# State-space scan and gated FFN on one core: reordered start of chunk 0

## The chip, the cores and the metric

The kernel runs on one core of a Trainium2 chip. The metric is the device time of one execution in microseconds (us). TensorE (PE), VectorE (DVE), ScalarE (ACT), GpSimd (POOL) and SyncE (SP) each run their own queue in program order and wait for one another by semaphores.

## The reference

```python
# x: 4 batches, 8 heads, 768 tokens, head size 32; B, C: state size 16; a: decay per token
for c in range(nc):                      # chunks of 32 tokens
    cum = cumsum(log(clip(a)))           # within the chunk
    M = einsum('bhin,bhjn->bhij', C, B) * exp(cum_i - cum_j) * causal
    y = M @ x + (C @ state) * exp(cum_i)
    state = exp(sum(la)) * state + sum_j B_j x_j exp(cum_end - cum_j)
h = y_as_tokens_by_256 @ w_in            # 3072 x 256 by 256 x 2048
out = (h * cos(h)) @ w_out               # 3072 x 2048 by 2048 x 256
```

The result of the scan, 3072 tokens by 256, is the input of a feed-forward block with 2048 hidden columns. All is float32. The chunk of 32 in the reference is only a way to compute the recurrence; the kernel may cut the sequence otherwise.

## The kernel before

**Tiling.** The sequence of 768 tokens is cut into NC = 6 chunks of P = 128. In each chunk, the scan of all four batches gives yT, the transposed y, and the feed-forward block of that chunk runs in NF = 16 steps. While a chunk's steps run, the scan of the next chunk is interleaved with them. Chunk 0 has nothing to be interleaved with, so its scan is cut into two units, k = 0 and 1, of W = 64 tokens, and the feed-forward steps of chunk 0 take turns: the even steps work on unit 0, the odd ones on unit 1 (`turn_of`). Steps 2j and 2j + 1 use the same hidden columns.

**One step n of the feed-forward block.** `first(n)` multiplies yT by four 128x128 blocks of w_in into hp (a PSUM bank, tag "h", two of them; hp n can only start when the bank of n - 2 has been read for the last time). `wind(n)` computes k, the number of turns as an integer, on ScalarE (L670), and w, the rest of a turn, on VectorE (L672). `gate(n)` takes the sine on ScalarE (L677, called cos in the text since it is shifted by a quarter turn), `gated(n)` multiplies by hp into gT on VectorE (L682). `second(n)` adds gT times w_out into o (L726 in chunk 0); it is called two steps later.

**The weights.** They arrive as 64-bit words in pieces, eight of w_in ("in", i) and eight of w_out ("out", i), and must be turned into float32. `grade(which, i)` is the first half: ScalarE takes |x| of the high words (L231) and a scaled copy of the low words (L229, tile last), and GpSimd clips |x| (L232). With `later=True` it returns the L229 part as `rest`, so that it can be put elsewhere in ScalarE's queue. `join(which, i)` is the second half: two VectorE instructions (L244, L246) and an add on GpSimd into w_in or w_out (L254). Piece i of either matrix holds the 256 hidden columns from 256i on. In chunk 0 these belong to the steps 2i and 2i + 1.

**The scan of chunk 0.** For unit k and batch half p, `spread_a` copies the decays over partitions by a small product on TensorE (L346, tile a_ps), and `decays0` runs the decay scan on VectorE (L356, tile lam). `turn_c` and `turn_b` transpose C and B on TensorE (L376, L390; tile tp), and ScalarE copies the results out (L380, L391). `reach0` is one product and one scan for the decay from the unit's start (L396, L398). `inner` forms C times B (L415, tile g), `weights` multiplies by lam (L424, tile m), `weigh0` and `weigh_c` scale B and C on GpSimd (L363, L406). `finish0` forms y: the part from the old state in unit 1 (L440), the part within the unit (L448), and then the sums of the new state (L458); ScalarE copies y into yT (L468, L466), and later `take` copies the state out (L476).

**What sets the order.** The program runs under a manual schedule: each engine gets its instructions in the order in which the Python code calls them. The order of the start is written out by hand below the helpers (L818 to L850) and in `first_steps` (L917), which covers steps 0 to 3. From step 4 on, a loop calls `first`, `wind`, `grade`, `gate`, `join` and `gated` of each step, with the piece given by `piece` (L869), and the scan's work of later chunks by the table `plan`. The loads are issued from SyncE's queue in the order of the code; only the loads of C of chunk 0 go from ScalarE's. The clipped decays are written to DRAM by `clips` (L860) and read back spread over partitions (arow), and the loads of later chunks are queued behind this.

Of the kernel before, what the change touches and what calls it, by code (L numbers as in the profile page):

```python
# [25 lines left out]
def kernel(  # L26
# [12 lines left out]
    nc = tc.nc  # L39
# [4 lines left out]
    P = 128  # L44
# [9 lines left out]
    W = P // 2  # L54
# [67 lines left out]
    def load_b(k, s, eng=nc.sync):  # L122

        eng.dma_start(out=bs[s * W:(s + 1) * W, k].rearrange("p q (h n) -> p (q h) n", h=H),
                      in_=B[2 * s:2 * s + 2, :, k * W:(k + 1) * W, :]
                      .rearrange("b h i n -> i (b h) n"))
# [133 lines left out]
    fetch("in", 0)  # L260
    for s in range(2):
        load_x(0, s)
    for s in range(2):
        load_b(1, s)
    fetch("in", 1)
    for s in range(2):
        load_x(1, s)
# [9 lines left out]
    quarter = const.tile([P, 1], FP32, name="quarter")  # L277
    V.memset(quarter, HALF_PI)
    ACT.activation(const.tile([P, 1], FP32, name="sine"), quarter, AF.Sin)
    V.memset(a0z[:, :, 0:1], 0.0)  # L280
    for r in (slice(NB * H, W), slice(W, P)):
        V.memset(a0z[r, :, 1:], 0.0)
# [67 lines left out]
    def decays0(k, p, i=0, n=1):  # L350

        if p == i == 0:
            lams[k] = scan.tile([P, 2, H, W], FP32, tag="lam", bufs=4, name="lam")
        flat = "p h i -> p (h i)"
        hs = slice(i * H // n, (i + 1) * H // n)
        V.tensor_tensor_scan(out=lams[k][:, p, hs].rearrange(flat),  # L356
                             data0=spread.pop((k, p, i)).rearrange(flat),
                             data1=unit0[:, hs].rearrange(flat), initial=0.0,
                             op0=ALU.mult, op1=ALU.add)
# [12 lines left out]
    def turn_c():  # L372

        tp = bank([P, 4, P], "tp", "o")
        for r in range(4):
            PE.transpose(tp[:, r], c0[:, r].rearrange("p h n -> p (h n)"), ident)  # L376
        tp = tp.rearrange("p r (b k g) -> p k b g r", b=NB, k=2)

        def of(k, dst, **v):
            ACT.activation(dst.rearrange("p b (g r) -> p b g r", r=4), tp[:, k], AF.Copy, **v)  # L380

        def take(k):
            for t in range(2):
                of(k, cuts[k][:, t].rearrange("p q (s i) -> p (q s) i", s=2), scale=slot[:, t:t + 1])
        return take, of
# [16 lines left out]
    def weigh_c(k, of):  # L402
        c = scan.tile([P, NB, W], FP32, tag="rT", name="c1")
        of(k, c)
        rTs[k] = t = scan.tile([P, NB, W], FP32, tag="rT", name="rT")
        G.tensor_tensor(out=t, in0=c, in1=reach1[:, :, 1:], op=ALU.mult)  # L406
# [17 lines left out]
        V.tensor_tensor(out=m, in0=gs[k, q][:, :, 0:2 * P].rearrange("p k (s i) -> p k s i", s=2),  # L424
                        in1=l, op=ALU.mult)

    def finish0(k):

        m, xk = units[k], xrs[k]
        y = [pair("y") for _ in range(2)] if k else [pair("y")]  # L430
        at_ = [[(y[t][:, s, p * W:(p + 1) * W] if k else
                 y[0][:, s, t * P + p * W:t * P + (p + 1) * W]) for p in range(2)]
               for t in range(2) for s in range(2)]
        if k:
            old = states0.pop(k)
            for p in range(2):
                for s in range(2):
                    for q in range(4):
                        r, c0 = slice(32 * q, 32 * q + 32), W * (q % 2)
                        PE.matmul(at_[2 * (q // 2) + s][p][c0:c0 + W], lhsT=old[r, s, p],  # L440
                                  rhs=rTs[k][r, 2 * p + s], start=(p == 0), stop=False,
                                  tile_position=(32 * q, c0), skip_group_check=True)
        for p in range(2):
            for t in range(2):
                for s in range(2):
                    ss = slice(s * W, (s + 1) * W)
                    for q in range(4):
                        PE.matmul(at_[2 * t + s][p][32 * q:32 * q + 32],  # L448
                                  lhsT=xk[ss, p, 4 * t + q], rhs=m[ss, p, 4 * t + q],
                                  start=(k == p == t == 0), stop=True,  # L450
                                  tile_position=(s * W, 32 * q), skip_group_check=True)
        sc = scs.pop(k).rearrange("p (q k h) n -> p q k (h n)", q=2, h=2)
        x2 = xk.rearrange("p q (k h) d -> p q k (h d)", h=2)
        for p in range(2):
            for s in range(2):
                ss = slice(s * W, (s + 1) * W)
                for q in range(4):
                    PE.matmul(y[0][32 * q:32 * q + 32, s, 3 * P + p * W:3 * P + (p + 1) * W],  # L458
                              lhsT=sc[ss, p, q], rhs=x2[ss, p, q], start=False, stop=True,
                              tile_position=(s * W, 32 * q), skip_group_check=True)  # L460
        if k == 0:
            yT[0] = two.tile([P, 2, 2, 2 * P], FP32, tag="yT", name="yT")
        t_ = yT[0][:, k]
        if k:
            for t in range(2):
                ACT.copy(out=t_[:, t].rearrange("p (s i) -> p s i", s=2), in_=y[t][:, :, 0:P])  # L466
        else:
            ACT.copy(out=t_.rearrange("p t (s i) -> p s t i", s=2),  # L468
                     in_=y[0][:, :, 0:2 * P].rearrange("p s (t i) -> p s t i", t=2))
        states0[k + 1] = new = states.tile([P, 2, 2, 2 * D], FP32, tag="state0", bufs=2,  # L470
                                           name="state0")

        def take():
            for t in range(2):
                ts = slice(t * D, (t + 1) * D)
                ACT.activation(new[:, :, :, ts], y[0][:, :, 3 * P:].rearrange(  # L476
                    "p s (q d) -> p s q d", q=2)[:, :, :, ts], AF.Copy, scale=slot[:, t:t + 1])

        def add():
            dec = scan.tile([P, 2, 2, 2 * D], FP32, tag="whole", bufs=1, name="whole")  # L480
            r4 = reach1.rearrange("p (q s) i -> p s q i", s=2)
            for s in range(2):
                G.tensor_tensor(out=dec[:, s], in0=old[:, s],
                                in1=r4[:, s, :, W:].to_broadcast([P, 2, 2 * D]), op=ALU.mult)
            G.tensor_tensor(out=new, in0=new, in1=dec, op=ALU.add)
            for u in range(2):
                state[0, u] = new[:, u].rearrange("p s (t d) -> p s t d", t=2)
        return take, add
# [176 lines left out]
            if between and e == 0:  # L665
                between()

    def wind(n):
        k = ffn.tile([P, TB], I32, tag="k", name="k")
        ACT.activation(k, hp[n], AF.Copy, bias=0.25, scale=INV_2PI)  # L670
        turns[n] = w = ffn.tile([P, TB], FP32, tag="w", name="w")
        V.scalar_tensor_tensor(out=w, in0=hp[n], scalar=INV_2PI, in1=k,  # L672
                               op0=ALU.mult, op1=ALU.subtract)

    def gate(n):
        cos = turns[n]
        ACT.activation(cos, cos, AF.Sin, bias=quarter, scale=TWO_PI)  # L677
# [144 lines left out]
    spread_a(0, 1, 0, 2, "h")  # L822
    for p, i in ((0, 0), (0, 1), (1, 0)):
        decays0(0, p, i, 2)
    take_c, of_c = turn_c()
    tp_b = bank([P, 4, P], "tp", "o")
    take_b = turn_b(0, tp_b)
    spread_a(0, 1, 1, 2, "h")
    decays0(0, 1, 1, 2)
    take_c(0)  # L830
    take_b()
    scan_reach = reach0(1)
# [6 lines left out]
    for q in range(2):  # L839
        weights(0, q)  # L840
    take_c(1)
    weigh_c(1, of_c)
    join("in", 0)
    take_s0, _ = finish0(0)
    take_b = turn_b(1, tp_b)
    take_b()
    spread_a(1, 1, tag="o")
    inner(1, 0)
    for p in range(2):
        decays0(1, p)  # L850
# [66 lines left out]
    def first_steps():  # L917

        take_s0()
        first(0, lambda: inner(1, 1))  # L920
        weigh0(1)
        rest = grade("in", 1, later=True)
        rest()
        units_of_decay()
        for q in range(2):
            weights(1, q)
        wind(0)
        rest = grade("out", 0, later=True)
        take_s1, add_s1 = finish0(1)
        join("in", 1)  # L930
        first(1)
        gate(0)
        rest()
        clips()
        gated(0)
        wind(1)
        join("out", 0)
        first(2)
        rest = grade("in", 2, later=True)
        gate(1)  # L940
        take_s1()
        rest()
        gated(1)
        second(0)
        wind(2)
        join("in", 2)
        first(3)
        rest = grade("out", 1, later=True)
        gate(2)
        rest()  # L950
        gated(2)
        second(1)
        wind(3)
        join("out", 1)
        rest = grade("in", 3, later=True)
        gate(3)
        rest()
        gated(3)
        rest = grade("out", 2, later=True)
        join("in", 3)  # L960
        rest()
        return add_s1

    add_s1 = first_steps()
# [86 lines left out]
```

## Time and profile before

| | |
|---|---|
| time, median of 3 runs | 379.91 us (379.07 to 380.12) |
| span of the profiled execution | 376.4 us |
| PE busy | 366.0 us, 97% |
| PE weight loads busy | 325.2 us, 86% |
| DVE busy | 281.6 us, 75% |
| POOL busy | 215.6 us, 57% |
| ACT busy | 172.6 us, 46% |
| hp (L663), 768 records | 184.2 us |
| o in chunks 1 to 5 (L764), largest of its groups | 65.8 us |

The busy shares are means over the whole span. The page also gives the chain of work that ended last: 76% of the span on TensorE, 11% on SyncE's queue, 6% on VectorE. A line of the timeline gives start, length, engine, line, operation, output and inputs, the number of merged instructions and, in brackets, how long the engine stood idle before it and what released it.

### The profile page before, as it was taken

What the parts mean: (1) busy time and instruction counts of PE and PEld (TensorE: products, weight loads), DVE (VectorE), ACT (ScalarE), POOL (GpSimd) and SP (SyncE); (2) the same over time, 40 slices, a digit from 0 to 9 for tenths busy, and PEclk for the clock granted to TensorE, in tenths of its full rate; (3) what the DMA queues carried; (4) which work ended last, traced back from release to release, by engine and by line L of the source; (5) the groups of instructions that cost most, each with busy time, mean ns of one, the idle gap of its engine ahead of it and who ended that gap; (6) DMA issues with size and microseconds to landing.
All of it is one profiled execution on the core that took longest, in us unless ns stands there. A gap on an engine that the chain in (4) does not pass through costs nothing.

```text
span 376.4 us, 8678 instructions
## 1 busy us (share of the span) xinstructions
PE 366.0 (97%) x3272; PEld 325.2 (86%) x3272; DVE 281.6 (75%) x470; ACT 172.6 (46%) x293; POOL 215.6 (57%) x334
## 2 busy tenths in 40 slices
PE   8989999999999999999999999999999999999995
PEld 4567877888899899999899999999999989999995
DVE  6867999889889957987767987776887872554543
ACT  3677566535344334344433445433444443444442
POOL 5555775489947545684454694363775344554451
PEclk9999999999999999999999999999999999999999
DMA  7988988314536641845213653211020000010011
GB/s 130 259 245 234 254 209 161 84 14 120 138 82 85 123 109 16 127 111 136 39 31 35 122 151 84 46 19 17 2 39 9 10 21 2 2 29 2 2 28 28
DMA packets 121353, 31.54 MB, mean 84 GB/s; under 512 B 90496, under 2 KB 117216, under 8 KB 121312
## 3 DMA queue, kind: packets, MB, share of 16 engines
q1 hardware_dynamic: 120064, 30.60, 37.9%
q8 instruction: 26, 0.43, 0.5%
q10 hardware_dynamic: 1248, 0.39, 0.4%
q14 instruction: 15, 0.12, 0.1%
HBM read 27.64 MB, written 3.34 MB: 82 GB/s over the span
## 4 chain that ended last, share of the span: by engine, by line
PE 76%; SPq 11%; DVE 6%; DMA 3%; issue 2%; POOL 1%; ACT 1%; DVEq 0%; ACTq 0%
PE hp L663 36%; PE o L764 29%; SPq L110 6%; SPq L155 3%; PE o L726 3%; PE y L602 2%; PE g L560 2%; PE y L595 1%; DMA arow<-a_cut 1%; PE a_ps L346 1%; DVE lam L510 1%; DVE mag L246 1%; DVE gT L682 1%; DVE w L672 1%; PE warm L84 1%
## 5 line engine op out<-in xcount | busy, mean ns | idle before, releaser
L663 PE MATMUL hp<-yT,w_in 128*128 128x256 f32 x768 | 184.2, 382 | 3.9 <-DVE gT L682 1.9
L663 PEld LDWEIGHTS hp<-yT,w_in 128*128 128x128 f32 x768 | 139.0, 190 | 24.9 <-issue 6.8
L707 POOL TENSOR_TENSOR gd<-gT 128x256 f32<-128x256 f32 x79 | 59.2, 749 | 98.9 <-DVE gT L682 97.1
L677 ACT ACTIVATE w<-w,quarter 128x512 f32<-128x512 f32 x96 | 69.2, 721 | 80.8 <-DVE w L672 80.8
L672 DVE SCALAR_TENSOR_TENSOR w<-hp,k 128x512 f32<-128x512 f32 x96 | 65.4, 682 | 42.3 <-ACT k L670 42.1
L670 ACT ACTIVATE k<-hp 128x512 int32<-128x512 f32 x96 | 57.2, 595 | 83.8 <-PE hp L663 83.6
L682 DVE TENSOR_TENSOR gT<-hp,w 128x512 f32<-128x512 f32 x96 | 65.2, 679 | 33.2 <-ACT w L677 24.3
L764 PE MATMUL o<-words,gd 128*128 128x128 f32 x474 | 65.8, 275 | 0.0
L764 PEld LDWEIGHTS o<-words,gd 128*128 128x128 f32 x474 | 59.2, 192 | 0.0
L510 DVE TENSOR_TENSOR_SCAN lam<-arow,unit 128x512 f32<-128x512 f32 x40 | 56.6, 1414 | 0.0
L764 PEld LDWEIGHTS o<-w_out,gT 128*128 128x128 f32 x316 | 47.5, 191 | 4.0
L710 POOL TENSOR_TENSOR gd<-gT,gd 128x128 f32<-128x128 f32 x79 | 44.6, 565 | 6.2
L764 PE MATMUL o<-w_out,gT 128*128 128x128 f32 x316 | 48.0, 274 | 0.0
L709 POOL TENSOR_TENSOR gd<-gT,gd 128x128 f32<-128x128 f32 x79 | 44.2, 559 | 6.2
L726 PE MATMUL o<-w_out,gT 128*128 128x256 f32 x128 | 30.4, 381 | 1.0 <-POOL w_out L254 1.0
L581 DVE TENSOR_TENSOR m<-g,lam 128x256 f32<-128x256 f32 x80 | 30.9, 415 | 0.5
L764 PE MATMUL o<-w_out,gd 128*128 128x128 f32 x158 | 30.6, 275 | 0.0
L764 PE MATMUL o<-words,gT 128*128 128x128 f32 x158 | 30.5, 275 | 0.0
L726 PEld LDWEIGHTS o<-w_out,gT 128*128 128x128 f32 x128 | 24.1, 190 | 4.9 <-POOL w_out L254 1.8
L764 PEld LDWEIGHTS o<-w_out,gd 128*128 128x128 f32 x158 | 24.0, 192 | 0.0
L764 PEld LDWEIGHTS o<-words,gT 128*128 128x128 f32 x158 | 24.0, 192 | 0.0
L781 DVE TENSOR_TENSOR sum<-ps,sum 128x256 f32<-128x256 f32 (+1 forms) x27 | 16.7, 644 | 0.6
(108 smaller groups left out, 267.2 us busy)
## 6 DMA issues: line engine op xcount, KB each, us to landing
arow<-a_cut SPq DMA_DIRECT2D x20, 512.0 KB
words<-in_moe_w_in_dram SPq DMA_DIRECT2D x8, 512.0 KB
words<-in_moe_w_out_dram SPq DMA_DIRECT2D x8, 512.0 KB
out_dram<-sum SPq DMA_DIRECT2D x18, 128.0 KB
blocks<-in_B_dram SPq DMA_DIRECT2D x128, 8.0 KB
blocks<-in_C_dram SPq DMA_DIRECT2D x128, 8.0 KB
xr<-in_x_dram SPq DMA_DIRECT2D x14, 128.0 KB
along<-a_all SPq DMA_DIRECT2D x20, 64.0 KB
```

Source lines behind the costliest of these rows:

```text
L510: V.tensor_tensor_scan(out=lam[c, b][:, hs].rearrange("p h i -> p (h i)"), data0=rows_.rearrange("p h i -> p (h i)"), data1=unit[:, b % 2 ...
L581: V.tensor_tensor(out=m_[js, :, :, is_], in0=g_[js, :, :, is_], in1=l_[js, :, :, is_], op=ALU.mult)
L663: PE.matmul(to_[:, e], lhsT=w_in[:, k, fs], rhs=y[:, k], start=(k == 0), stop=(k == KT - 1), skip_group_check=True)
L670: ACT.activation(k, hp[n], AF.Copy, bias=0.25, scale=INV_2PI)
L672: V.scalar_tensor_tensor(out=w, in0=hp[n], scalar=INV_2PI, in1=k, op0=ALU.mult, op1=ALU.subtract)
L677: ACT.activation(cos, cos, AF.Sin, bias=quarter, scale=TWO_PI)
L682: V.tensor_tensor(out=gT[n], in0=hp.pop(n), in1=cos, op=ALU.mult)
L707: G.tensor_tensor(out=d[:, 0:2], in0=g[:, 1:2].to_broadcast([P, 2, P]), in1=g[:, 3::-3], op=ALU.subtract)
L709: G.tensor_tensor(out=d[:, 2], in0=g[:, 0], in1=d[:, 0], op=ALU.subtract)
L710: G.tensor_tensor(out=d[:, 3], in0=g[:, 2], in1=d[:, 2], op=ALU.subtract)
L726: PE.matmul(o[c, u][:, t], lhsT=g[:, 2 * e + t], rhs=w_out[:, 2 * j + e], start=(j == e == t == 0), stop=(j == NJ - 1 and e == 1), skip_gr ...
L764: PE.matmul(at[q], lhsT=a_[q], rhs=w[q], start=(j == 0 and q in starts), stop=(j == NJ - 1), skip_group_check=True)
```

## The change

It changes only the start: the scan of chunk 0 and the steps 0 to 3.

- In `finish0`, the sums of the new state come ahead of the part of y within the unit, which has to wait for m. A hook `between` lets the caller put work between these products and the copies into yT.
- In the order of the start, the last product `spread_a(0, 1, 1, ...)` and its scan come ahead of the transposes of C and B; `join("in", 0)` ahead of `weigh_c`; `spread_a(1, 1)` ahead of `turn_b(1)`.
- One of the four loads of B moves from SyncE's queue to ScalarE's.
- `wind` is split in its ScalarE and its VectorE half. In `first_steps`, the pieces are graded and joined earlier: out-1 is graded ahead of wind 2 instead of behind it, in-3 is graded in step 2 instead of step 3, and joined in step 3 ahead of the last part of out-2 instead of at the step's end.

```diff
-    for s in range(2):
-        load_b(1, s)
+    load_b(1, 0)
...
+    load_b(1, 1, nc.scalar)
...
-    def finish0(k):
+    def finish0(k, between=None):
...
+        sc = scs.pop(k).rearrange("p (q k h) n -> p q k (h n)", q=2, h=2)
+        x2 = xk.rearrange("p q (k h) d -> p q k (h d)", h=2)
+        for p in range(2):
+            for s in range(2):
+                ss = slice(s * W, (s + 1) * W)
+                for q in range(4):
+                    PE.matmul(y[0][32 * q:32 * q + 32, s, 3 * P + p * W:3 * P + (p + 1) * W],
+                              lhsT=sc[ss, p, q], rhs=x2[ss, p, q], start=(k == p == 0), stop=True,
+                              tile_position=(s * W, 32 * q), skip_group_check=True)
...
-                                  start=(k == p == t == 0), stop=True,
+                                  start=False, stop=True,
...
-        sc = scs.pop(k).rearrange("p (q k h) n -> p q k (h n)", q=2, h=2)
...
+        if between:
+            between()
...
+    spread_a(0, 1, 1, 2, "h")
+    decays0(0, 1, 1, 2)
     take_c, of_c = turn_c()
     tp_b = bank([P, 4, P], "tp", "o")
     take_b = turn_b(0, tp_b)
-    spread_a(0, 1, 1, 2, "h")
-    decays0(0, 1, 1, 2)
...
+    join("in", 0)
     weigh_c(1, of_c)
-    join("in", 0)
     take_s0, _ = finish0(0)
+    spread_a(1, 1, tag="o")
     take_b = turn_b(1, tp_b)
     take_b()
-    spread_a(1, 1, tag="o")
...
-        rest = grade("in", 1, later=True)
-        rest()
+        grade("in", 1)
         units_of_decay()
         for q in range(2):
             weights(1, q)
-        wind(0)
+        take_s1, add_s1 = finish0(1, lambda: wind_k(0))
+        join("in", 1)
+        wind_w(0)
+        first(1)
         rest = grade("out", 0, later=True)
-        take_s1, add_s1 = finish0(1)
-        join("in", 1)
-        first(1)
         gate(0)
         rest()
         clips()
         gated(0)
+        join("out", 0)
         wind(1)
-        join("out", 0)
         first(2)
         rest = grade("in", 2, later=True)
         gate(1)
...
         gated(1)
         second(0)
+        grade("out", 1)
+        join("in", 2)
         wind(2)
-        join("in", 2)
         first(3)
-        rest = grade("out", 1, later=True)
+        rest = grade("in", 3, later=True)
         gate(2)
+        join("out", 1)
         rest()
         gated(2)
         second(1)
         wind(3)
-        join("out", 1)
-        rest = grade("in", 3, later=True)
+        rest = grade("out", 2, later=True)
         gate(3)
+        join("in", 3)
         rest()
         gated(3)
-        rest = grade("out", 2, later=True)
-        join("in", 3)
-        rest()
```

More of the change, by code (lines that the diff above doesn't have):

```diff
@@ L449, in finish0 @@
                                   lhsT=xk[ss, p, 4 * t + q], rhs=m[ss, p, 4 * t + q],
-                                  start=(k == p == t == 0), stop=True,
+                                  start=False, stop=True,
                                   tile_position=(s * W, 32 * q), skip_group_check=True)
-        sc = scs.pop(k).rearrange("p (q k h) n -> p q k (h n)", q=2, h=2)
[L453 to L460, printed above, removed]
         if k == 0:
@@ L666, in first, with wind_k, wind_w @@
                 between()
-    def wind(n):
+    def wind_k(n):
         k = ffn.tile([P, TB], I32, tag="k", name="k")
         ACT.activation(k, hp[n], AF.Copy, bias=0.25, scale=INV_2PI)
+        turns[n] = k
+    def wind_w(n):
+        k = turns[n]
         turns[n] = w = ffn.tile([P, TB], FP32, tag="w", name="w")
@@ L673, in wind @@
                                op0=ALU.mult, op1=ALU.subtract)
+    def wind(n):
+        wind_k(n)
+        wind_w(n)
     def gate(n):
```

## The prediction

> **What bounds the kernel now.** I read the table of stretches first, because the page's averages mix a short start with a long steady part.
>
> ```profile
> core 0: us, PE busy (x) PEld busy (x) DVE busy (x) ACT busy (x) POOL busy (x), PEclk, DMA share, GB/s
> ...
> 10.00:20.00 10.00, 9.43 (x278) 6.39 (x277) 8.04 (x12) 6.74 (x16) 5.69 (x9) 1.00 1.00 281
> 20.00:30.00 10.00, 8.27 (x37) 6.50 (x36) 5.87 (x11) 6.95 (x14) 5.40 (x8) 1.00 0.87 229
> 30.00:40.00 10.00, 9.43 (x43) 7.70 (x42) 8.45 (x11) 5.64 (x10) 7.22 (x7) 1.00 0.81 216
> 40.00:50.00 10.00, 9.44 (x44) 7.71 (x43) 9.70 (x15) 7.43 (x13) 8.01 (x9) 1.00 0.93 249
> 50.00:60.00 10.00, 9.67 (x47) 8.23 (x46) 9.90 (x12) 5.51 (x10) 6.36 (x7) 1.00 0.84 208
> ```
>
> From 140 us on PE is full (59.94 of 60 us, then 99.95 of 100): nothing the diff edits lies there. Before that PE has holes: 0.57 us in 10-20, 1.73 in 20-30, 0.57, 0.56 and 0.33 in the next three. In 20-30 VectorE (DVE) is idle 4 us; from about 33 to 65 it is never free. So I read the start as three regimes: waits in a chain up to 33 us, VectorE from 33 to 65, TensorE after that. A microsecond won by 33 us comes out at the end only if both later regimes move up with it.
>
> Second view: the timeline, for which wait ends last at 25 to 37 us.
>
> ```profile
> 30.99 1.28 POOL L254 TENSOR_TENSOR w_out<-mag,last 128x512 uint32<-128x512 uint32 x1 [2.38 <-DVE mag L246]
> 31.01 0.68 ACT L231 ACTIVATE mag<-words 128x512 f32<-128x512 f32 x1
> ...
> 32.23 1.20 POOL L232 TENSOR_SCALAR mag<-mag 128x512 f32<-128x512 f32 x2
> ...
> 32.33 1.99 PE L726 MATMUL o<-w_out,gT 128*128 128x256 f32 x8 [0.51 <-POOL w_out L254]
> ...
> 32.88 0.82 DVE L244 TENSOR_SCALAR mag<-mag 128x512 uint32<-128x512 uint32 x1 [1.45 <-POOL mag L232]
> ...
> 34.35 0.68 DVE L672 SCALAR_TENSOR_TENSOR w<-hp,k 128x512 f32<-128x512 f32 x1
> 34.52 1.27 POOL L254 TENSOR_TENSOR w_in<-mag,last 128x512 uint32<-128x512 uint32 x1 [1.09 <-DVE mag L246]
> 34.95 1.12 DVE L244 TENSOR_SCALAR mag<-mag 128x512 uint32<-128x512 uint32 x1
> ...
> 37.01 0.68 DVE L682 TENSOR_TENSOR gT<-hp,w 128x512 f32<-128x512 f32 x1
> ```
>
> Piece in-3 is graded last in step 3: its |x| leaves ScalarE at 31.7, its clip stands behind out-1's add on GpSimd (to 32.27), and VectorE waits 1.45 us for it. TensorE loses 0.51 us to out-1 itself. Everything of step 4 (w at 34.35, gT at 37.01) stands behind these two in-order queues, and hp 7 and later take their PSUM bank from gT two steps back. The lane is then saturated with waits for GpSimd written into it: L244 takes 1.12 us here beside a GpSimd add, 0.42 elsewhere.
>
> Third view: the starts of hp, whose pitch would be 3.46 us (1.73 each for hp and o) if TensorE never waited. hp 6 starts at 37.84, hp 13 at 65.73. From the first o at 24.64 to hp 13 TensorE has 21 groups of 1.73, turns of 0.44 and a scan product of 0.81, 37.6 us of work in 41.1: 3.5 us of waiting is all that can be won there.
>
> **What the skill says, and the trace.** "SBUF — State Buffer", section "SBUF: two separate sides", says that VectorE with two SBUF inputs or in certain modes and GpSimd hold a shared port pair exclusively, so one blocks. The 1.12 against 0.42 us above agrees. "TensorE: Matmul & The Clock Gate", "What's actually happening", gives a half-rate clock until some 3.4 us of activity: the first six a_ps products go at 0.43 us each from 3.92 on, the next two, at 7.47, at 0.29 (0.58 until the next group starts at 8.05). "Architectural detail" of the same page calls ScalarE and VectorE strictly first in, first out; the gaps above are that. "DMA: Bandwidth & Descriptors", "Issuing engines are not separate DMA queues", says another issuing engine saves only issue time; I use that for the moved load.
>
> **Part by part.** Times "now" are the timeline's; "then" is my propagation, each instruction starting at the later of its queue and its inputs.
>
> *a_ps of (1,1) ahead of the transposes.* tp of c starts at 6.67, as c arrives (6.61). Two more products go ahead of it: 2 x 0.21 = 0.43 us warm, 0.86 us if the clock is still at half. I take warm and 0.33 us of delay, since tp has some slack: take_c at 7.70 (now 7.36), g at 9.02 (now 8.69). VectorE gets its fourth scan at 7.3 instead of 8.17, but m needs g, whose first half is there at 9.4: m starts at 9.45, now 9.48. Nothing won, nothing lost; cold 0.4 us lost.
>
> *State sums ahead of y, unit 0.* They run before m is ready, filling the 0.27-0.8 us that TensorE stood before y. But g and a_ps(1,0) are 0.33 late, so TensorE runs through to 11.75; now it is done with both at 11.73. yT at 11.9 in both. In unit 1 nothing separates them: 0.
>
> *join in-0 ahead of weigh_c.* w_in at 11.9 to 13.2 instead of 12.31 to 13.57. hp 0 doesn't come then (next item): 0.
>
> *spread_a(1,1) ahead of turn_b(1).* The second scan of VectorE starts at 12.94 instead of 13.28. But TensorE now turns b after the 1.0 us product, at 12.8; ScalarE copies it at 13.25-13.62; g(1,0) at 13.82 (now 13.16). The product that used to cover that copy is gone: hp 0 at 14.42 (now 13.76), y of unit 1 at 17.14 (16.48), hp 1 at 19.45 (18.75). **Cost 0.7 us.**
>
> *load_b(1,1) on ScalarE's queue.* Each of the first loads of B takes 0.73 us of issue (1.46 for two), each C load on ScalarE 0.61. ScalarE is free from 4.71 to 7.70, so 0 if it takes that. But the load at 5.34 on SyncE took 2.72 us to issue while the DMA share of its stretch, 5 to 8 us, stood above 1.0. If ScalarE's is as slow and begins when C has landed (5.9), it ends at 8.6 and take_c slips by 0.9. I take 0, and keep 0.9.
>
> *The new order of steps 0 to 3.* k of 0 goes at 17.22, w 0 at 18.0 behind join in-1 (two instructions, 0.41 + 0.69). grade out-0 now follows yT: |x| at 19.65, cos of 0 at 20.25 (now 18.86), gT 0 at 20.95 (now 19.63). join out-0 moves ahead of w 1: w_out at 22.85-24.15, so the first o starts at 24.2 instead of 24.64. **Gain 0.45.** Then o 0, hp 3, o 1 at 1.73 each end at 29.4.
>
> grade out-1, both ScalarE instructions, now stands ahead of k 2: a new wait. Behind cos 1 (24.1) come the state copies (0.6), last of in-2, |x| and last of out-1 (0.59 each), so k 2 starts at 26.5 though hp 2 is done at 23.5; now it starts at 24.22. w 2 follows at 27.15, out-1's two at 27.8, gT 2 at 28.9-29.6 (now 26.52). hp 4, which takes gT 2's bank, starts at 29.7; TensorE was busy to 29.4, so 0.3 us of this long wait is felt. Now hp 4 is at 29.93.
>
> What it buys: w_out of out-1 at 29.0-30.3 (now 30.99-32.26), so o 2 follows hp 4 at 31.45 (now 32.32). in-3's pair on VectorE at 30.4-31.55, in front of gT 3 (31.55-32.2), clipped at 27.85 already: the wait of 1.45 is gone. k 4 comes at 31.7 (hp 4 ends at 31.45, last of out-2 ahead of it), w 4 at 32.35 instead of 34.35, **2.0 us earlier**. in-3's GpSimd add is over at 32.95, before out-2's VectorE pair (33.0-34.1), which no longer meets it: gT 4 at 34.1 instead of 37.01, **2.9 us earlier**. hp 6 at 36.65 (now 37.84).
>
> *33 to 65 us.* The same VectorE instructions in the same order. TensorE alone would reach hp 13 at 36.65 + 7 x 3.46 + 0.44 + 0.81 = 62.1, 3.6 us ahead of 65.73. VectorE in its present, contended pace keeps between its 2.0 and its 2.9. So hp 13 is 2.0 to 2.9 early: 2.45.
>
> *Loads.* SyncE issues without pause from 21.9 to about 128 us, so data don't move up with the work. By the clips (then 20.9-21.9, now 20.86-21.9) they start at the same time. The first broadcast row is issued at 26.80; one later took 4.58 us to land, so 31.4, needed at 34.8. The blocks issued up to 111.5 are needed at 124.5, 122 then. A lead of 3 us is inside each of these.
>
> After 65 us TensorE is bound and keeps the lead. 379.9 - 2.4 = **377.5 us**.
>
> **Rivals.** (a) *VectorE keeps up fully*: with the in-3 collision gone its pairs slip between GpSimd's, and TensorE's 3.6 us come out: 376.3. For it: instructions at their short times sum to less than TensorE's pitch, except in the four steps with a 1.9 us scan. Against it: 9.90 of 10 busy in 50-60. (b) *The wait only moves*: k 2 behind grade out-1, plus the late start, make w 4 no earlier than the 1.2 us that hp 6 wins less a slip of 0.9, or VectorE gives most of it back in collisions: 0.3 won, 379.6. For it: the slack of hp 4 is only 0.3 us. (c) *Slower*: cold products 0.4, the slow load 0.9 and the swap's 0.7 make 2.0 before step 1, which cancels the 2.0 of w 4; and |x| of in-3, asked for at 27.1 on ScalarE's one queue instead of 31.01, has to wait for its words. If these came only at 31.0, cos 2 would go at 31.6, gT 2 at 32.3-33.0, hp 4 at 33.1, 3.4 later than above, so w 4 at 35.75, 1.4 behind now: 381.3. For it: the page has DMA at its fullest just when these words move. Against it: in-3 was issued at 15.54, ahead of in-4, and some 5.3 MB asked for by 17 us, at the 229 to 281 GB/s of the table, are over by 26.
>
> **How the numbers follow.** Forecast 0.49, (a) 0.15, (b) 0.17, (c) 0.19. Faster by over 0.3% means under 378.8: forecast and (a), 0.64. Same is (b), 0.17; slower 0.19. The low end lies under (a)'s 376.3 by the scatter of 0.3, at 376.0; the high end takes in (b) and the mild part of (c), where only one of the unknown 0.4 and 0.9 comes: 380.6.
>
> **What would show it.** Right: g(1,0) and hp 1 later by 0.7, first o near 24.2, k 2 near 26.5 with about 3 us behind hp 2, no VectorE wait at the last piece of the four steps, w 4 near 32.4, gT 4 near 34.1, hp 13 near 63.3, equal spacing after. Wrong: a ScalarE take_c past 8 us; hp 1 past 20; |x| of in-3 released by a DMA; hp 13 no earlier than 65 although w 4 is, which would put the fault in the VectorE stretch; or the lead gone between 65 and 130, which would put it in the loads.

## The result and the profile after

| | before | after |
|---|---|---|
| first comparison, median (n) | 379.76 us (4; 379.07 to 380.12) | 375.49 us (4; 375.12 to 376.58) |
| ratio, 95% interval | | 0.9895 (0.9869 to 0.992) |
| second comparison, median (n) | 378.49 us (17) | 375.35 us (6; 375.00 to 375.53) |
| ratio, 95% interval | | 0.9906 (0.9889 to 0.9923) |
| span of the profiled execution | 376.4 us | 373.6 us |
| hp 1, hp 13 start at | 18.76, 65.68 us | 19.20, 62.87 us |

The change is worth 4.3 us in the first comparison, 3.1 in the second and 2.8 between the two traces. To read these three one needs to know that executions of the kernel before fall into two groups, which no run here explains: of the 86 timed beside the experiments, 55 had a mean granted TensorE clock of 0.998 to 1.000 and took 377.9 to 379.4 us (median 378.3), and 31 had 0.989 to 0.994 and took 379.65 us and more (median 380.0). Against the 55 the change wins 378.3 - 375.4 = 2.9 us, what the traces show.

The lines from which hp 1 and hp 13 are read, two of the kernel before and two of the changed one (the first merges hp 1 with the first six products of hp 2):

```profile
18.76 3.63 PE L663 MATMUL hp<-yT,w_in 128*128 128x256 f32 x14 [0.46 <-ACT yT L466]
65.68 1.99 PE L663 MATMUL hp<-yT,w_in 128*128 128x256 f32 x8
```

```profile
19.20 1.99 PE L665 MATMUL hp<-yT,w_in 128*128 128x256 f32 x8 [0.33 <-ACT yT L468]
62.87 1.99 PE L665 MATMUL hp<-yT,w_in 128*128 128x256 f32 x8
```

From hp 13 to the end of the span it takes 310.7 us in both: what is won by hp 13 is kept to the end.

The table of stretches of the changed kernel (columns as before the change):

```profile
10.00:20.00 10.00, 8.96 (x276) 5.99 (x275) 7.00 (x11) 5.10 (x14) 5.15 (x7) 1.00 1.06 293
20.00:30.00 10.00, 9.04 (x40) 7.08 (x39) 7.57 (x13) 8.71 (x17) 7.32 (x10) 1.00 0.78 205
30.00:40.00 10.00, 10.00 (x48) 8.79 (x48) 9.52 (x14) 7.50 (x13) 6.57 (x8) 1.00 0.85 234
40.00:50.00 10.00, 10.00 (x48) 8.81 (x47) 9.90 (x13) 7.14 (x12) 8.66 (x10) 1.00 0.91 246
```

In 20-30 VectorE does 1.7 us more than before (7.57 against 5.87): the pieces are taken up there. In 30-50 TensorE has no hole left, where it had 1.13 us. In 10-20 it is worse by 0.47, and hp 1 starts 0.44 us later: the start is no better.

The timeline of the changed kernel, at the places shown of before (now `w` is L678, `gT` L692, `o` L736):

```profile
28.88 1.28 POOL L254 TENSOR_TENSOR w_out<-mag,last 128x512 uint32<-128x512 uint32 x1 [0.63 <-DVE mag L246]
29.54 1.96 PE L665 MATMUL hp<-yT,w_in 128*128 128x256 f32 x8 [0.15 <-DVE gT L692]
29.91 0.53 DVE L244 TENSOR_SCALAR mag<-mag 128x512 uint32<-128x512 uint32 x1
31.34 1.89 PE L736 MATMUL o<-w_out,gT 128*128 128x256 f32 x8
31.54 1.28 POOL L254 TENSOR_TENSOR w_in<-mag,last 128x512 uint32<-128x512 uint32 x1 [0.62 <-DVE mag L246]
32.17 0.69 DVE L678 SCALAR_TENSOR_TENSOR w<-hp,k 128x512 f32<-128x512 f32 x1
32.78 0.42 DVE L244 TENSOR_SCALAR mag<-mag 128x512 uint32<-128x512 uint32 x1
34.14 0.68 DVE L692 TENSOR_TENSOR gT<-hp,w 128x512 f32<-128x512 f32 x1
```

Out-1's add on GpSimd is 2.11 us earlier, in-3's 2.98, and o 2 at 31.34 no longer waits for w_out. L244 of in-3 has no bracket: VectorE's wait of 1.45 us is gone. w 4 comes 2.18 us earlier, gT 4 2.87. The wait that took their place is the 0.15 us of hp 4 for gT.

### The profile page after: what moved, and what is told of

Same layout as the page of the kernel before. It is cut to its first block, busy times and chain, and to the rows that moved or that the text cites. A ratio compares the mean times of both kernels' runs of the same rounds, so it can differ in the third digit from the quotient of the medians.

```text
span 373.6 us, 8681 instructions
## 1 busy us (share of the span) xinstructions
PE 363.9 (97%) x3272; PEld 325.2 (87%) x3272; DVE 280.8 (75%) x470; ACT 172.6 (46%) x293; POOL 215.2 (58%) x334
## 4 chain that ended last, share of the span: by engine, by line
PE 72%; DVE 11%; POOL 6%; DMA 3%; issue 3%; SPq 2%; ACT 1%; POOLq 0%; DVEq 0%; ACTq 0%
PE hp L665 35%; PE o L774 30%; POOL words L711 3%; DMA xr<-in_x_dram 3%; PE y L604 2%; DVE mag L246 2%; DVE gT L692 2%; DVE w L678 2%; PE g L562 2%; DVE mag L244 1%; DVE lam L512 1%; POOL gd L717 1%; PE y L597 1%; DVE m L583 1%; POOL gd L719 1%
## 5 line engine op out<-in xcount | busy, mean ns | idle before, releaser
L678 DVE SCALAR_TENSOR_TENSOR w<-hp,k 128x512 f32<-128x512 f32 x96 | 65.5, 682 | 38.3 <-ACT k L672 37.9
L692 DVE TENSOR_TENSOR gT<-hp,w 128x512 f32<-128x512 f32 x96 | 65.3, 680 | 35.9 <-ACT w L687 27.1
L736 PE MATMUL o<-w_out,gT 128*128 128x256 f32 x128 | 30.3, 380 | 0.0
L736 PEld LDWEIGHTS o<-w_out,gT 128*128 128x128 f32 x128 | 24.2, 190 | 3.4 <-POOL w_out L254 0.2
```

Of the source, the lines that this page charges most:

```text
L692: V.tensor_tensor(out=gT[n], in0=hp.pop(n), in1=cos, op=ALU.mult)
L736: PE.matmul(o[c, u][:, t], lhsT=g[:, 2 * e + t], rhs=w_out[:, 2 * j + e], start=(j == e == t == 0), stop=(j == NJ - 1 and e == 1), skip_gr ...
```

## The experiments

Two measures come from the traces: from tp of c to hp 1 (the start) and from hp 1 to hp 13 (the steps). The landing of C, after which GpSimd copies c, scatters from 5.91 to 6.57 us between executions and moves everything behind it; these differences leave it out. What they don't leave out is x, which lands while unit 0's sums run: the changed kernel's trace names a wait of 0.25 us for it at 10.82, and in other traces the first 28 products of the sums take up to 0.81 us instead of 0.51, which I put down to the same.

| kernel | time, median (n), us | tp of c to hp 1 | hp 1 to hp 13 |
|---|---|---|---|
| before | 378.3 (55, as above) | 12.09 | 46.92 |
| new step order alone | 375.27 (11) | 12.08 | 43.63 |
| new start alone | 378.7 (14) | 11.96 | 46.92 |
| after | 375.49 (4), 375.35 (6) | 12.46, 12.29 | 43.67, 43.65 |
| after, turn_b(1) first | 374.83 (6) | 11.49 | 43.64 |

**The kernel before, once more.** No edit; it tells what two measurements of one kernel differ by.

> The kernel before once more, to see how far one program scatters. The two traces differ by 2.8 us of span, the timed medians by 4.3. Theory A (the gain is the 2.8 of the traces, the rest is scatter of the kernel before): span within 1 us of 376.4 in most executions, ratio to before 1.000. Theory B (the profiled execution of before was a lucky one): spans mostly at 377.5 to 378.5, and the profile taken now shows where the extra 1.5 us lie.

378.36 us (22 executions), ratio 0.9997 (0.9981 to 1.0014). Theory A holds: 16 of the 22 have a span of 376.1 to 377.2 us; the other six lie at 378.0 to 378.6, where theory B had most of them. A ratio that differs from 1 by 0.15% tells nothing.

**The new step order alone.** The kernel before with the new `first_steps`, and what that calls:

```diff
-    def finish0(k):
+    def finish0(k, between=None):
...
-    def wind(n):
+    def wind_k(n):
...
+        take_s1, add_s1 = finish0(1, lambda: wind_k(0))
...
+        grade("out", 1)
...
+        rest = grade("in", 3, later=True)
...
```

> The kernel before with the new order of the steps 0 to 3 and the hook alone; the scan of chunk 0, its loads and the sums stay as before. Theory A (the gain comes from out-1 and in-3 being taken up earlier, and the new start only costs, mostly by the swap of the product and the turn of b): hp 1 at 18.75, the first o at 23.4 to 24.0, hp 13 at 62.3 to 62.9, so a time 0 to 0.6 us below the changed kernel, 4 us below before. Theory B (the new start pays as well): at most 2.5 us below before.

375.27 us, ratio 0.9913 (0.9888 to 0.9939). hp 1 to hp 13 takes 43.63 us instead of 46.92, the 43.67 of the whole change. So the step order holds all of the gain. Theory A has hp 13 right (62.61 us); of its 4 us below before 3.1 came. Four of the 11 executions lie at 376.03 us and more, of which the section on the prediction tells; the other seven have a median of 375.02, some 0.4 below the changed kernel.

**The new start alone.** The changed kernel with the old `first_steps`:

```diff
-        take_s1, add_s1 = finish0(1, lambda: wind_k(0))
+        wind(0)
+        rest = grade("out", 0, later=True)
+        take_s1, add_s1 = finish0(1)
...
```

> The changed kernel with the old order of the steps 0 to 3. Theory A: the start costs 0.4 to 0.7 us at hp 1, which the wait for the clip of in-3 passes on: 0.3 to 0.7 us slower than before. Theory B (the start pays): 1 us or more faster than before.

378.7 us (378.14 to 379.22), ratio 0.9995 (0.9976 to 1.0015). The ratio hides a loss, since 13 of the 40 executions of before beside it took 379.65 us and more and none of these 14 did. Against the other 27 (median 378.2) and the 16 alike of the measurement above (378.3) the new start is 0.4 to 0.5 us slower, as theory A had it. The trace, of an execution of 378.30 us, does not show where: from tp of c to hp 1 it takes 0.13 us less than before, and hp 13 starts at 65.72 instead of 65.68. A later landing of C or of x in most executions would fit; it is not shown.

**turn_b(1) ahead of spread_a(1,1) again.** The changed kernel with one swap undone:

```diff
-    spread_a(1, 1, tag="o")
     take_b = turn_b(1, tp_b)
     take_b()
+    spread_a(1, 1, tag="o")
```

> The changed kernel with the turn of b of unit 1 ahead of the second product of unit 1 again. Theory A (TensorE's chain through the turn, its copy and the scan products sets hp 0 and hp 1): g of unit 1 at 13.2 instead of 13.76, hp 1 at 18.6 instead of 19.20, and 0.4 to 0.6 us off the end. Theory B (VectorE's second scan, 0.34 us earlier by the swap, sets them): no gain, or 0.3 us lost.

374.83 us (374.17 to 375.33), ratio 0.989 (0.9855 to 0.9926), some 0.5 us better than the change in time and trace, as theory A had it; no other version has a lower median. Its timeline against that of the changed kernel:

```profile
11.63 1.08 PE L346 MATMUL a_ps<-m,those 128*64 128x512 f32 x4
11.87 0.38 ACT L391 COPY turned<-tp 128x256 f32<-128x256 f32 x1
12.63 0.67 PE L415 MATMUL g<-cT,turned 32*64 32x128 f32 x16
13.23 1.13 PE L665 MATMUL hp<-yT,w_in 128*128 128x256 f32 x4
```

```profile
11.85 1.08 PE L346 MATMUL a_ps<-m,those 128*64 128x512 f32 x4
12.86 0.44 PE L390 MATMUL tp<-ident,bc 128*128 128x128 f32 x2
13.76 0.67 PE L415 MATMUL g<-cT,turned 32*64 32x128 f32 x16 [0.46 <-ACT turned L391]
14.36 1.13 PE L665 MATMUL hp<-yT,w_in 128*128 128x256 f32 x4
```

With the transpose first, ScalarE's copy runs while TensorE is at the a_ps product, and g follows that product without a bracket. With the product first TensorE stands 0.46 us for the copy. From the copy of yT to hp 0 it takes 1.84 us (11.39 to 13.23) and 2.37 (11.99 to 14.36): the swap costs 0.53.

**The changed kernel again, beside the next runs.** No edit.

> The changed kernel once more, on the same chip as the kernel before and the three variants below. The theory that the step order gains 3.3 us and the start with its swap nothing: 375.3 to 375.6 against 378.4 for the kernel before, 2.8 to 3.1 less. The rival that the first comparison was right in full, 4.3 us: 374.1 or less.

375.35 us against 378.49: 3.1 less, as the first theory has it. The 4.3 us of the first comparison did not come again.

**The sums behind y again.** From here on each edit starts from the variant with turn_b(1) first.

```diff
-                              lhsT=sc[ss, p, q], rhs=x2[ss, p, q], start=(k == p == 0), stop=True,
...
-                                  start=False, stop=True,
+                                  start=(k == p == t == 0), stop=True,
...
+                              lhsT=sc[ss, p, q], rhs=x2[ss, p, q], start=False, stop=True,
```

> As the variant with turn_b(1) ahead of spread_a(1,1), but the products of the sums stand behind those of y again. If putting the sums first pays in the start, yT of unit 0 comes 0.2 to 0.4 us later after POOL's c and the whole is 0.2 to 0.4 slower than that variant's 374.8. The rival is my forecast's 0: the sums only change places with y in front of the same copies, and the two agree within 0.1 us.

375.12 us (374.90 to 376.27). From tp of c to hp 1 it takes 11.99 us instead of 11.49, of which 0.16 is a named wait for x; hp 1 stands 0.46 instead of 0.33 us for yT of unit 1. That leaves 0.34: the traces say that the sums ahead pay some 0.3 us, as the theory had it. The times, 375.12 against 374.83, point the same way but overlap.

**Loads of along on ScalarE.**

```diff
-            nc.sync.dma_start(
+            (nc.scalar if c >= 3 else nc.sync).dma_start(
                 out=along[c][:, b], in_=a_all[b, :, c * P:(c + 1) * P].unsqueeze(1)
```

> As the variant with turn_b(1) ahead of spread_a(1,1), but the loads of the transposed C for chunk 3 are issued by ScalarE instead of SyncE. If SyncE's row of issues is what makes the last blocks of chunk 3 nearly late, the four loads of blocks for its second unit are issued about 4 us earlier than their 177.4, VectorE's transposes of blocks near 180 never wait, and no execution lies 1.4 to 1.7 us above the others: all within 0.6 us, 374.2 to 374.9. The rival: ScalarE pays the 6 issues at 0.6 to 0.7 each ahead of its own copies and the kernel is 0.5 to 2 us slower than 374.8.

(Along holds the decays, read back from a_all, not C as the expectation says, and the edit moves these loads for the chunks 3 to 5.)

382.6 us (381.81 to 383.70), ratio 1.0103 (1.0081 to 1.0126): a miss of both. From hp 13 to the end it takes 317.9 us instead of 310.7: the loss lies there. ScalarE's own row shows the largest wait:

```profile
170.91 1.22 ACTq L174 DMA_DIRECT2D along<-a_all  x2
172.23 0.60 ACT L672 ACTIVATE k<-hp 128x512 int32<-128x512 f32 x1 [9.08 <-DMA along<-a_all]
```

ACTq is ScalarE issuing a load. The pair took 1.22 us to issue, but ScalarE had been idle since 163.15 and the issue did not begin until 170.91; k, behind it, came after 9.08 us. What held the issue the trace doesn't name. With such a loss the run can't tell what SyncE's row is worth; an edit that leaves ScalarE alone follows below.

**k of step 2 ahead of out-1's second half on ScalarE.**

```diff
-        grade("out", 1)
+        rest = grade("out", 1, later=True)
         join("in", 2)
         wind(2)
+        rest()
```

(The expectation speaks of VectorE; the instruction that the edit moves, L229, is ScalarE's.)

> As the variant with turn_b(1) ahead of spread_a(1,1), but the last VectorE instruction of grade out-1 stands behind wind(2) instead of ahead of it. If k of step 2 standing behind that piece costs time, k comes 0.5 to 0.6 us earlier after the first o, hp4 no longer waits for gT, and the whole gains 0.1 to 0.5 us on 374.8. The rival: TensorE is busy without a gap from 30 us on in either case, so only hp4's 0.15 us can be won and the time stays within 0.15 us.

374.94 us; hp 1 to hp 13 takes 43.67 us. k 2 does come earlier, 6.17 us after hp 1 instead of 6.71, and still nothing is won:

```profile
24.58 0.60 ACT L672 ACTIVATE k<-hp 128x512 int32<-128x512 f32 x1
25.43 1.27 POOL L254 TENSOR_TENSOR w_in<-mag,last 128x512 uint32<-128x512 uint32 x1
25.82 1.17 DVE L244 TENSOR_SCALAR mag<-mag 128x512 uint32<-128x512 uint32 x1
27.93 0.68 DVE L692 TENSOR_TENSOR gT<-hp,w 128x512 f32<-128x512 f32 x1
28.75 1.53 PE L665 MATMUL hp<-yT,w_in 128*128 128x256 f32 x6 [0.16 <-DVE gT L692]
```

Between w 2 and gT 2 stand two VectorE instructions of out-1. With k 2 earlier the first of them runs beside an add of GpSimd (L244 takes 1.17 us instead of 0.59), and gT 2 comes when it came before, 9.52 us after hp 1 (9.49). Hp 4 waits its 0.16 us as ever. The rival was right.

**Chunk 4's B and x behind chunk 3's blocks.**

```diff
-            if c > 0 and f == (NJ if c == 1 else 0):
+            if c > 0 and f == (NJ if c == 1 else NJ - 1 if c == 2 else 0):
```

> As the variant with turn_b(1) ahead of spread_a(1,1), but the twelve loads of B and x for chunk 4 stand behind the blocks of chunk 3 in SyncE's row of issues, not ahead of them; every other engine's row is the same. If SyncE's row of issues is what brings chunk 3's last blocks nearly late, those four loads are issued 6 to 8 us earlier than their 175.1, the transposes of blocks never wait for a load, and at the full granted clock no execution lies over 0.7 us above the lowest: 374.2 to 374.9. The rival: the executions that are 1.2 to 1.7 us longer have another cause, and some at full clock still come at 375.7 to 377.

374.89 us (374.26 to 375.57). The last four loads of blocks for chunk 3 are issued at 167.23 instead of 175.12, VectorE uses them at 180.07: a margin of 10.5 us after the last issue. No execution reaches the 375.96 us from which the late loads described below are counted. The highest lies 1.3 us over the lowest, not 0.7 as forecast; C's landing alone moves the start by some 0.7 (it is at its latest, 6.57, in this trace). Six executions don't prove that none would be late; the margin does more. What it prevents is seen in the next run.

**a_ps(1,1) behind the transposes again.**

```diff
-    spread_a(0, 1, 1, 2, "h")
-    decays0(0, 1, 1, 2)
     take_c, of_c = turn_c()
     tp_b = bank([P, 4, P], "tp", "o")
     take_b = turn_b(0, tp_b)
+    spread_a(0, 1, 1, 2, "h")
+    decays0(0, 1, 1, 2)
```

> As the variant with turn_b(1) ahead of spread_a(1,1), but the products a_ps(1,1) of unit 0 stand behind the transposes of C and B again. My forecast held that moving them ahead costs 0.33 us and wins 0.33: then from POOL's c to hp1 it takes the same 12.16 us within 0.1, and so does the whole, 374.8. What the changed kernel's trace suggests instead: ahead of the transposes the products are done before POOL's c and cost nothing, so behind them they add their two passes, 0.2 to 0.45 us, to the start and to the whole: 375.0 to 375.3.

375.21 us. From tp of c to the first g it takes 2.02 us; with the products ahead it is 1.84 or 1.85 in every trace. So moving them wins 0.18 us, just under the lower edge of the second theory. To hp 1 it takes 11.78, against 11.43 to 11.54 in four traces of the same start with the products ahead and 11.79 in two where x stretches the sums by 0.3; here x stretches them by 0.12. The profiled execution, of 377.74 us, also has a stall that the traces of two other edits have too:

```profile
178.77 1.89 PE L665 MATMUL hp<-yT,w_in 128*128 128x256 f32 x8
179.07 2.31 SPq L155 DMA_DIRECT2D blocks<-in_C_dram  x4
182.99 0.45 DVE L526 STREAM_TRANSPOSE turned<-blocks 128x256 f32<-128x256 f32 x1 [2.69 <-DMA blocks<-in_C_dram]
184.43 0.91 PE L562 MATMUL g<-cT,turned 32*64 32x256 f32 x32 [2.21 <-ACT cT L546]
185.93 1.97 PE L665 MATMUL hp<-yT,w_in 128*128 128x256 f32 x8 [0.59 <-DVE gT L692]
```

The same place in the changed kernel:

```profile
175.59 2.60 SPq L155 DMA_DIRECT2D blocks<-in_C_dram  x4
180.34 0.74 DVE L526 STREAM_TRANSPOSE turned<-blocks 128x256 f32<-128x256 f32 x2
```

SyncE issues the last four loads of C's blocks 3.5 us later; VectorE stands 2.69 us for them, g stands for VectorE, and two hp that lie 4.35 us apart otherwise lie 7.16 apart. The trace of the new step order alone, an execution of 376.7 us, has the same stall ahead of 181.85, 1.38 us long, and that of the sums behind y (376.27 us) one of 1.24 ahead of 181.40. In these three traces VectorE goes on 1.5 to 1.7 us after the end of the last issue, so that much a load needs. The margin, from the end of the last issue to the use, was 4.6 us before (178.56 to 183.16) and is 2.15 now: SyncE's row issues with hardly a pause and came only some 0.4 us earlier, the work 2.8. Where the row falls behind can be followed by one issue: that of along near 55 us comes at 55.2 in the variant with turn_b(1) first and at 59.4 here, and 4.0 us of these 4.2 are still there at the pair of along near 174 (173.76, 177.79). Of the 4.2 us, 0.73 are there at the first issue after clips (20.22, 20.95), as the whole start is later in this trace; the rest arises between 22 and 56 us, and nothing later makes it good.

**in-3 and out-2 one place later.**

```diff
-        rest = grade("in", 3, later=True)
         gate(2)
         join("out", 1)
-        rest()
         gated(2)
...
-        rest = grade("out", 2, later=True)
+        rest = grade("in", 3, later=True)
         gate(3)
-        join("in", 3)
         rest()
         gated(3)
+        rest = grade("out", 2, later=True)
+        join("in", 3)
+        rest()
```

> As the variant with turn_b(1) ahead of spread_a(1,1), but the pieces in-3 and out-2 are taken up one place later, as in the kernel before: in-3 in step 3 and not in step 2, out-2 behind gated(3). If the gain of the new step order comes from VectorE no longer standing idle before a piece that POOL and ScalarE have still to prepare, VectorE's busy share in 28 to 36 us falls below 0.99 again and hp1 to hp13 takes 44.3 to 45.5 us instead of 43.64: 375.4 to 376.7. The rival: all of it was won by step 2 already, by k and w of the first steps coming earlier; then hp1 to hp13 stays within 0.3 of 43.64 and the time at 374.8 to 375.1.

375.87 us, 1.0 above its base; hp 1 to hp 13 takes 44.64 us. The theory was right, save that VectorE's share from 28 to 36 us is below 0.99 in the base as well (0.98 there, 0.84 here; rows below).

**out-1 later as well.** From that last kernel:

```diff
-        grade("out", 1)
-        join("in", 2)
         wind(2)
+        join("in", 2)
         first(3)
+        rest = grade("out", 1, later=True)
         gate(2)
-        join("out", 1)
+        rest()
         gated(2)
         second(1)
         wind(3)
+        join("out", 1)
```

> As the variant with in-3 and out-2 one place later, but piece out-1 too is taken up as in the kernel before: behind first(3), not ahead of wind(2). Steps 2 and 3 are then those of the kernel before, and only the steps 0 and 1 and the start are new. If the gain lies in filling VectorE's idle time behind the first o with a whole piece, out-1 is the larger part: hp1 to hp13 goes from 44.64 us back to 46.3 to 46.9, and the time to 377.5 to 378.1. The rival: k and w of steps 0 and 1 are the larger part, and hp1 to hp13 stays at 44.6 to 45.6, the time at 375.9 to 376.9.

377.21 us (376.94 to 377.61); hp 1 to hp 13 takes 45.93 us, between what the two theories had. Undone in this order, the gain of the step order comes in three parts of like size: 46.92 - 45.93 = 0.99 us from steps 0 and 1, 45.93 - 44.64 = 1.29 from out-1, 44.64 - 43.64 = 1.00 from in-3 and out-2. One row of the tables shows it: the stretch from 28 to 36 us of, in this order, the kernel before, this one, the one above, and the variant with turn_b(1) first.

```profile
28.00:36.00 8.00, 7.49 (x35) 6.29 (x34) 5.39 (x8) 5.57 (x10) 4.53 (x7) 1.00 1.05 278
```

```profile
28.00:36.00 8.00, 7.47 (x35) 6.27 (x34) 5.99 (x9) 6.03 (x11) 5.51 (x7) 1.00 1.03 273
```

```profile
28.00:36.00 8.00, 8.00 (x39) 6.87 (x38) 6.70 (x10) 6.39 (x11) 6.21 (x7) 1.00 0.94 263
```

```profile
28.00:36.00 8.00, 7.86 (x37) 6.76 (x36) 7.81 (x12) 5.42 (x9) 5.91 (x6) 1.00 0.92 239
```

VectorE's busy time (the third figure with a count) climbs from 5.39 to 7.81 of 8 us, though the starts of the four lie up to 1 us apart. TensorE looks no better in the last than in the third (7.86 against 8.00): what VectorE has done by 36 us is felt later. From hp 6 to hp 9 the third takes 11.17 us (35.55 to 46.72), the last 10.36 (35.37 to 45.73).

## Why the prediction was wrong

The direction, the place and the mechanism were right; the time, 375.49 us, lies below the range, whose low end was 376.0. The step that failed is the last one of the sum, 379.9 - 2.4: its first term.

**The base.** The forecast took 2.4 us from 379.9, the median given. The page that every step was read from was of an execution of 378.18 us. The steps could only be right for that one: 378.18 - 2.45 = 375.7, 0.2 above what was measured. With 1.7 us off, the range would have been 374.3 to 378.9. Two of the three times behind that median, 379.91 and 380.12, lie where the 31 executions with the lower clock lie; their own clocks aren't on record, so that this is the reason is argued, not shown. This term, 1.7 us, is by itself the miss. The gain itself was put too low by less: 2.81 us at hp 13, not 2.45.

**The new order of steps 0 to 3, and 33 to 65 us.** Right. Hp 1 to hp 13 was to become 43.85 us from 46.98, and is 43.67 from 46.92. The step by step times hold within some 0.5: first o 24.2 (23.97), k 2 26.5 (25.99), hp 4 29.7 (29.54), o 2 31.45 (31.34), w 4 32.35 (32.17), gT 4 34.1 (34.14), hp 6 36.65 (36.52), hp 13 63.3 (62.87). VectorE kept a lead of 2.8, near the upper of the two values between which the middle was taken. That k 2 behind out-1 makes hp 4 wait was half right: 0.3 us was taken and 0.15 came, and the run with k 2 earlier shows that VectorE's row, not ScalarE's, sets gT 2. That the lead is kept after 65 us was right (310.7 us from hp 13 to the end in both).

**spread_a(1,1) ahead of turn_b(1).** Right in mechanism: 0.7 was taken, 0.53 measured.

**a_ps of (1,1) and the sums, both put at 0.** Mis-sized: they win about 0.2 and 0.3 us, which pays for the swap. The start lost not 0.7 but, by the three traces that have the whole of it, -0.13 to 0.37 (11.96, 12.29, 12.46 against 12.09), the largest with the named wait for x in it; by the times of the new start alone it lost some 0.4. The 0.33 of delay for tp did not come: the products were done at 6.26, before c.

```profile
3.92 2.34 PE L346 MATMUL a_ps<-m,those 128*64 128x256 f32 x16
6.74 0.66 PE L376 MATMUL tp<-ident,c 128*128 128x128 f32 x4 [0.48 <-POOL c L323]
```

TensorE even stands 0.48 us for c. In the trace of before, six products at 0.43 us each lasted up to 6.6; here they go at 0.21 or 0.22 from the third of the eight on, which I read as the clock's rise (last section). In other executions it came later, and tp started up to 0.25 us behind c's end (7.44 against 7.19) where it follows within 0.07 if the products are done.

**join in-0 and load_b on ScalarE, at 0.** The 0.9 us feared did not come: the load took 0.73 us to issue on ScalarE, at 3.36, and cT's copy started at 7.43 and 7.49 us in the two traces of the change. (It passed 8 us, at 8.01 and 8.14, only where C came last and the products ran longest, so that sign did not tell what it was meant to.) Whether C lands a little later with the load there (GpSimd's c at 5.93, 5.99 and 6.24 us in three traces with the old start, at 5.91 to 6.57 with a median of 6.23 in eleven with the new one) stays open; the load wasn't moved alone. It is one candidate for the 0.4 us that the new start loses.

**Loads.** "A lead of 3 us is inside each of these" was checked up to the blocks needed at 124.5; the loads behind those were put at nothing without a look. At 180 us the margin, 4.6 us before, is 2.15, and of the 49 executions of the kernels with the whole new step order and the loads where they were (two with a clock of 0.995 left out), 10 took 375.96 us or more. Three of these were the profiled ones, and each has the stall, 1.24, 1.38 and 2.69 us long, and takes 1.5, 1.6 and 2.8 us more than 310.7 from hp 13 to the end; that it is the cause in the other seven is argued. The medians move little by it: without these executions 375.02 instead of 375.27 for the new step order alone, 374.96 instead of 375.21 for a_ps(1,1) behind the transposes.

**The rivals.** (a) at 376.3 was the nearest, by the same base: with 378.18 it would have read 374.6, 0.8 too low. (b) and (c) did not come: |x| of in-3 waited for no load, and no stretch gave the lead back.

## What to carry to other kernels

Subtract a gain read from a profile from the time of the execution that was profiled, not from a median of other runs; where the two differ by more than the scatter, find out why before adding them up. In a start that is a chain of in-order rows, fill the engine that will later be the bound (here VectorE) as early as its inputs can be had, and expect the gain where that engine is saturated, not where the edit is. After moving work earlier, follow the row of issues to the end of the program: the smallest margin may lie a hundred microseconds on.

## What was not expected of the hardware

- The time at which TensorE's clock rises differs between executions of the same instructions. The eight a_ps products (16 records) that start at 3.92 us took 2.34 us in the changed kernel's trace (0.21 or 0.22 each from the third on) and 3.59 in that of the kernel with chunk 4's loads moved (0.42 to 0.48 throughout), though up to there the two kernels' instructions are the same. The Trainium skill, "TensorE: Matmul & The Clock Gate", section "What's actually happening", says so: the window is free-running, and one kernel shows different numbers of cold products. The traces agree.
- SyncE's row of issues is a resource of its own. "DMA: Bandwidth & Descriptors", section "Issuing engines are not separate DMA queues", calls the time to initiate a DMA "usually small relative to the DMA itself". Here eight loads of 8 KB took 4.60 us to issue, 0.58 each, against the 1.5 to 1.7 us that passed in the three stalls from the end of the last issue to VectorE's next instruction: smaller, but a row of them adds up. In the changed kernel SyncE never stood for more than 0.94 us between two issues from 22 to 200 us.
